# Attention, router and two mixture-of-experts layers on one core: first small loads from ScalarE, noise loads in steps of their own, and a new table for the order of the attention's steps

## The chip, the cores and the metric

The kernel runs on one core of one Trainium2 chip. A core has five engines that run side by side and wait for each other through semaphores: TensorE (PE, matrix products), VectorE (DVE), ScalarE (ACT), GpSimd (POOL) and SyncE (SP, which here only issues transfers). Sixteen DMA engines move the data between the chip's memory and the core's on-chip memory. Every engine works through its own list of instructions strictly in order, so an instruction that waits also holds up all that stands behind it on its engine.

The metric is the device time of one execution in microseconds (us). About 0.3% of it, some 4 us, is what a measurement of this kernel can tell from no change.

## What is computed

The reference has three parts. Only the first, and the routing that follows from it, is touched by the change.

```python
def _attn_ref(q, k, v, g_norm):            # (8, 8, 576, 64) each
    kv = np.einsum('bhsd,bhse->bhde', k, v)
    out = np.einsum('bhsd,bhde->bhse', q, kv)
    rms = np.sqrt(np.mean(out * out, axis=-1, keepdims=True) + 1e-06)
    return (out / rms * g_norm)

x = attn_out.transpose(0, 2, 1, 3).reshape(4608, 512)

def _moe_ref(x, w_gate, w_noise, noise, w1, w2):   # 8 experts, 512 -> 1024 -> 512
    noisy = x @ w_gate + np.log1p(np.exp(x @ w_noise)) * noise
    # the two best experts of each row, weights by softmax over the two,
    # out[row] += weight * (relu(x[row] @ w1[e]) @ w2[e])

def _moe2_ref(x, w_skip, w_gate, w1, w2):  # rows with x @ w_skip > 0: the best expert
    ...                                    # of 8 is added, times its probability
```

## The kernel before

**Three stages.** The attention stage comes first. For each batch b it forms k^T v per head (TensorE, `kv_half`, twice per batch with 4 heads each), then q times that product. The rows of the result are written to `xrows` in memory. Beside it the router picks two experts for each row, in two halves of 4 batches (`route_half`). Then the first expert layer runs, expert by expert, and last the second one. From the first tile of the first expert layer on, the lists of instructions of the two kernels are the same on every engine; the change lies in the stage ahead of it and in the passage between.

**How the attention stage is laid out.** It is a list of 56 steps, `subs`: each is two or three heads of one half batch of q, and after every pair of batches come two steps for the 64 last rows of both. In the steps from `FIRST` = -6 to 56 the loop does, in this order: `run(i, 0)`, `q_transposed` for the step two ahead, `run(i, 1)`, `out_sub` of the step itself, `run(i, 2)`. So `run` has three slots per step, and whatever is filed with `at(step, f, ..., slot)` is written out there. All engines but the order between them are fixed by this: the code is emitted under a manual schedule, so each engine's list is the order in which this loop emits. What is filed where is set by tables of numbers at the top of the file:

- `KV`, `GC`: how many steps ahead of a batch's first step its two `kv_half` run, and where the two parts of `gate_columns` go. `gate_columns` appends 32 columns to the block `kvbd` of the batch, so that the product with q gives the router's logits too: first, TensorE transposes the sums `sw` (L447) and ScalarE copies them out (`kvT`, L449); second, TensorE multiplies them by the gate weights (L453) and ScalarE copies the columns into `kvbd` (L456, two instructions). The batch's first `out_sub` (L486) needs those columns.
- `QTE`, `OSBE`, `SQE`, `LOX`: which engine does each copy of transposed q (`qTs`, L471 or L473), each copy of a result out of PSUM (`osb`, L495 or L497), each square (`sq`, L500 or L502) and the low half of each row (`x`, L538).
- `FIN`, `FINR`: at which later step the normalisation, the logits (`stage3`), the two halves of the rows (`stage4` on ScalarE, L535; `stage5`, L538) and the write of the rows are emitted. Whatever falls behind step 56 goes into the list `late` and is worked off at `f` in the table `TAIL`.
- `WSTEPS`: the first expert's weights; each matrix is loaded (2 MB, `stage`), squared and summed by ScalarE in four pieces (`wjunk`, L175), summed by TensorE (L182, which waits for VectorE's `wsum`, L179), scaled and split.
- `ROUTE`: the 27 parts of the router's first half. The second half and four early tiles of expert 0 are woven together by `EPLAN` and `TAIL`, behind the last steps.
- `LOADS`, `CLEAR`: the remaining first loads, and nine 1 MB writes of zeros to the output.

**Loads.** All loads of the stage are issued by SyncE, in the order of the list. `km` and `vm` (half a batch of k or v, 512 KB each) have three buffers, `qm` has four, `kl`, `vl`, `ql` (the last 64 rows) two. A load of the next half batch is filed `LATER` = 4 steps behind the use that frees its buffer. Behind the first batches SyncE issues the noise of the router, six small loads (L397, L400), and one row of zeros, `null`, to `xrows` (L402).

## Time and profile before

| | us |
|---|---|
| median of 3 runs | 1263.92 |
| lowest and highest of them | 1261.89, 1265.8 |
| the profiled execution, its own time | 1256.98 |
| its span, first to last instruction | 1254.8 |
| TensorE busy in the span | 1176.7 (94%) |
| VectorE, ScalarE, GpSimd busy | 815.3, 656.2, 401.2 |
| granted TensorE clock, mean over the span | 0.98 of full |

The profiled execution is 2.2 us longer than its span and lies 6.9 us below the median of the runs. The busy share of TensorE is an average over the stages: in the expert layers it is at nearly 100%, in the attention stage it is not, and the attention stage is where the granted clock falls below full. So the share by itself doesn't tell what a microsecond saved in the attention stage is worth. What tells it is which wait ends last there, engine by engine, and where the stage hands over to the first full tile of expert 0.

### The profile page before, as it was taken

Reading aid. Unit: us, or ns where it says so; the run is one execution under the profiler, and the core shown is the slowest. Engines: PE = TensorE matmul, PEld = TensorE weight load, DVE = VectorE, ACT = ScalarE, POOL = GpSimd, SP = SyncE. Lnnn points to the kernel's source line nnn. Section 1 sums busy time; section 2 is a strip of 40 time slices with the busy share of each in tenths; the row PEclk is TensorE's granted clock in tenths of the full one; section 3 lists DMA queues with packets and bytes.
Section 4 is the critical chain, followed back from the end, with each engine's and each line's share of the span. In section 5 each row is a group of like instructions: output and inputs, shape, how many; then the busy total and the mean of one; then the engine's idle time right before and its main releaser. Section 6 shows DMA issues by size and latency. Waiting matters only on the chain.

```text
span 1254.8 us, 25287 instructions
## 1 busy us (share of the span) xinstructions
PE 1176.7 (94%) x9341; PEld 838.0 (67%) x9341; DVE 815.3 (65%) x2998; ACT 656.2 (52%) x1187; POOL 401.2 (32%) x477
## 2 busy tenths in 40 slices
PE   6977889999999999999999999999999989999996
PEld 5877777576767676766667576666666666666664
DVE  1777977344786777787777878778787765433321
ACT  2787561356655755574666767557774332222210
POOL 2564552112233232324242233232323331422220
PEclk8998899999999999999999999999999999999998
DMA  9999894678995988799799899979996673795680
GB/s 223 306 308 319 261 257 108 178 210 240 245 292 125 271 270 211 199 244 301 143 305 266 245 328 259 291 209 257 305 295 224 157 215 120 207 328 162 205 247 16
DMA packets 311410, 293.34 MB, mean 234 GB/s; under 512 B 205022, under 2 KB 256222, under 8 KB 307180
## 3 DMA queue, kind: packets, MB, share of 16 engines
q1 hardware_dynamic: 288316, 208.22, 62.7%
q0 software_dynamic: 22384, 82.36, 19.2%
q8 instruction: 75, 1.23, 0.4%
q10 hardware_dynamic: 576, 1.05, 0.3%
q14 instruction: 59, 0.48, 0.1%
HBM read 172.86 MB, written 93.42 MB: 212 GB/s over the span
## 4 chain that ended last, share of the span: by engine, by line
PE 52%; issue 14%; DVE 12%; ACT 11%; POOL 4%; DMA 2%; SPq 2%; another core or an unknown queue 1%; POOLq 0%; ACTq 0%; DVEq 0%
PE b L273 27%; PE a L234 20%; ACT wa L192 2%; ACT wjunk L175 2%; DVE xh L959 2%; ACT hh L242 2%; ACT wb L192 1%; ACT presplit L192 1%; POOL out_dram L1232 1%; PE kvps L421 1%; ACT ysb L1129 1%; DVE x L1133 1%; DVE hl L243 1%; POOL x2r L1187 1%
## 5 line engine op out<-in xcount | busy, mean ns | idle before, releaser
L234 PEld LDWEIGHTS <-wa 128*128 128x128 f16 x5184 | 458.5, 99 | 59.2 <-issue 10.3
L234 PE MATMUL a<-xT,wa 128*128 128x256 f16 (+6 forms) x3648 | 386.8, 266 | 6.7 <-issue 4.5
L273 PE MATMUL b<-wb,hh 128*128 128x512 f16 x1488 | 338.8, 379 | 6.1 <-ACT hh L242 6.1
L273 PEld LDWEIGHTS <-hh 128*128 128x128 f16 x1488 | 140.4, 98 | 167.0 <-ACT hh L242 14.2
L242 ACT ACTIVATE hh<-a 128x512 f16<-128x512 f32 (+5 forms) x186 | 107.1, 578 | 185.1 <-PE a L234 155.2
L243 DVE SCALAR_TENSOR_TENSOR hl<-a,hh 128x512 f16<-128x512 f32 (+5 forms) x186 | 124.9, 674 | 83.4 <-ACT hh L242 77.2
L273 PE MATMUL b<-wb,hl 128*128 128x512 f16 x744 | 175.7, 379 | 0.0
L1075 POOL DMA_INDIRECT xg<-xrows,idxp x67 | 65.6, 978 | 329.5 <-DVE orow L1099 285.2
L273 PEld LDWEIGHTS <-hl 128*128 128x128 f16 x744 | 72.2, 98 | 88.3 <-DVE hl L243 2.9
L1129 ACT ACTIVATE ysb<-b,gate 128x512 f32<-128x512 f32 x73 | 49.7, 681 | 125.8 <-PE b L273 69.0
L234 PE MATMUL a<-x2Tr,wa 128*128 128x256 f16 (+1 forms) x1152 | 109.0, 257 | 2.7 <-DMA x2Tr<-xh 2.7
L1137 POOL DMA_INDIRECT out_dram<-x,oi x67 | 68.3, 1020 | 133.2 <-DVE pi L1045 60.8
L175 ACT ACTIVATE wjunk<-stage 128x1024 bf16<-128x1024 f32 x96 | 101.2, 1054 | 2.0
L193 DVE SCALAR_TENSOR_TENSOR presplit<-stage,wscl,presplit 128x1024 f16<-128x1024 f32 x64 | 80.5, 1278 | 15.9 <-ACT presplit L192 15.0
L1108 POOL DMA_INDIRECT yo<-ydram,gi x67 | 69.9, 1043 | 51.1 <-issue 17.1
L192 ACT ACTIVATE presplit<-stage,wscl 128x1024 f16<-128x1024 f32 x64 | 71.2, 1140 | 18.2 <-DVE wscl L185 16.8
L951 ACT ACTIVATE jk<-x 128x512 bf16<-128x512 f32 x67 | 42.2, 629 | 54.9 <-DVE x L1133 46.7
L958 ACT ACTIVATE xh<-x,x2ss 128x512 f16<-128x512 f32 x67 | 45.4, 714 | 32.7 <-DVE x2ss L141 29.5
L486 PE MATMUL b<-kvbd,qTs 128*128 128x160 f32 x256 | 49.8, 332 | 9.8 <-issue 4.0
L1133 DVE TENSOR_TENSOR x<-ysb,yo 128x512 f32<-128x512 f32 x67 | 46.3, 691 | 18.6 <-ACT ysb L1129 14.4
L1232 POOL DMA_INDIRECT out_dram<-ysb,mrow x16 | 16.3, 1018 | 119.0 <-DVE ysb L1230 119.0
L421 PE MATMUL kvps<-vm,km 128*128 128x128 f32 x256 | 39.7, 320 | 12.7 <-DMA vm<-in_v_dram 9.4
(357 smaller groups left out, 1564.9 us busy)
## 6 DMA issues: line engine op xcount, KB each, us to landing
stage<-in_moe_w_dram SPq DMA_DIRECT2D x32, 2048.0 KB
wsd<-presplit SPq DMA_DIRECT2D x8, 2056.0 KB
ydram<-ysb SPq DMA_DIRECT2D x64, 256.0 KB
wsd<-presplit SPq DMA_DIRECT2D x8, 2048.0 KB
out_dram<-zeros SPq DMA_DIRECT2D x9, 1024.0 KB
km<-in_k_dram SPq DMA_DIRECT2D x16, 512.0 KB
vm<-in_v_dram SPq DMA_DIRECT2D x16, 512.0 KB
qm<-in_q_dram SPq DMA_DIRECT2D x16, 512.0 KB
```

What stands on the lines that cost most here:

```text
L175: A.activation(junk, st[:, F * c:F * c + F], AF.Square, accum_out=acc[:, c:c + 1], **kw)
L192: A.activation(hi[:, d], st[:, d], AF.Copy, scale=sc)
L193: V.scalar_tensor_tensor(lo[:, d], st[:, d], sc, hi[:, d], op0=ALU.mult, op1=ALU.subtract)
L234: PE.matmul(ps[:, i, :], a[:, c, fs], xT[:, b + c, 0:nt], start=(n == 0), stop=(n == 11))
L242: behind[0] = A.activation(hh[:, fsl, 0:nt], ps, AF.Relu).ins
L243: i = V.scalar_tensor_tensor(hl[:, fsl, 0:nt], ps, 0.0, hh[:, fsl, 0:nt], op0=ALU.max, op1=ALU.subtract)
L273: PE.matmul(ps, a[:, f, gsl], b[:, f, :], start=(fs.start == 0 and i == 0), stop=(fs.stop == 8 and a is hl and f == 7))
L1075: G.indirect_dma_start(out=xg[:, g], out_offset=None, in_=xrows, in_offset=bass.IndirectOffsetOnAxis(ap=idx[:, t0 + g:t0 + g + 1], axis=0))
L1108: G.indirect_dma_start(out=yo, out_offset=None, in_=ydram[0:BASE[e], :], in_offset=bass.IndirectOffsetOnAxis(ap=gi[:, g:g + 1], axis=0), b ...
L1129: A.activation(ysb, ps, AF.Copy, scale=gate[:, g:g + 1])
L1133: i = V.tensor_add(x2[:, g], ysb, yos[g])
L1137: s = G.indirect_dma_start(out=out, out_offset=bass.IndirectOffsetOnAxis(ap=oi[:, g:g + 1], axis=0), in_=x2[:, g], in_offset=None, bounds_ ...
```

## The change

It does four things.

1. SyncE's list begins with k and v. The loads that stood ahead of or between them (`gcol`, `kl` and `vl` of the first two batches, the gate weights `gw`) are issued by ScalarE, whose list had nothing but a table load there.
2. The six noise loads and the row of zeros, which SyncE issued in a row behind the third k and v, are filed at the steps of a new table `NOIS`.
3. The tables that set the order of the attention's steps have other numbers.
4. With them, single copies change engine: `OSBE` gives ScalarE 49 of 56 where it had 40, `QTE` 37 where it had 31, `SQE` still 38; `LOX` gives GpSimd 9 of 20 where it had 10.

```diff
-CLEAR = (51, 42, 49, 40, 46, 36, 53, 50, 41)
+CLEAR = (53, 53, 44, 44, 41, 35, 47, 42, 39)
...
-KV, GC = ((6, 3), ((3, 2), (0, 1)))
+KV, GC = ((6, 3), ((1, 0), (0, 0)))
-FIN = ((1, 0), (1, 1), (2, 0), (3, 1), (4, 1), (5, 2))
-FINR = ((1, 2), (1, 2), (2, 1), (3, 2), (6, 0), (8, 0))
+FIN = ((1, 2), (1, 2), (2, 0), (4, 1), (4, 2), (5, 1))
+FINR = ((1, 1), (1, 2), (1, 2), (5, 1), (6, 2), (8, 0))
-LOADS = (0, 1, 1, 1, -2, 20)
+LOADS = (-2, 3, 3, -2, -2, 12)
+NOIS = (16, 17, 18, 20, 21, 22, 23)
...
-WSTEPS = ((4, 12, 12, 13, 14, 15, 15, 15, 16, 18), (20, 24, 26, 27, 29, 29, 30, 35, 35, 38))
+WSTEPS = ((4, 11, 13, 14, 14, 14, 16, 16, 17, 18), (19, 24, 25, 25, 29, 29, 30, 38, 38, 39))
...
     gcol = const.tile([P, 1], F32, name="gcol")
-    SP.dma_start(gcol[0:64], g_norm.rearrange("(p o) -> p o", o=1))
-    SP.dma_start(gcol[64:128], g_norm.rearrange("(p o) -> p o", o=1))
...
-        def load_rest(nm, src, pb):
+        def load_rest(nm, src, pb, eng=SP):
...
-        load_rest("k", k, 0)
-        load_rest("v", v, 0)
+        load_rest("k", k, 0, A)
+        load_rest("v", v, 0, A)
         load_kv(1)
         load_q(0)
+        for c in range(2):
+            A.dma_start(gcol[64 * c:64 * c + 64], g_norm.rearrange("(p o) -> p o", o=1))
...
-        SP.dma_start(gw[:, :, 0:8], w_gate.rearrange("(c p) e -> p c e", p=P))
-        SP.dma_start(gw[:, :, 8:16], w_noise.rearrange("(c p) e -> p c e", p=P))
+        A.dma_start(gw[:, :, 0:8], w_gate.rearrange("(c p) e -> p c e", p=P))
+        A.dma_start(gw[:, :, 8:16], w_noise.rearrange("(c p) e -> p c e", p=P))
...
+        def load_noise(a, bl):
+            if bl is None:
+                SP.dma_start(noi[:, a, 0:16].rearrange("p (b r) e -> p b (r e)", r=4),
+                             nv[a, :, 0:512].rearrange("b (p r) e -> p b (r e)", r=4))
+            else:
                 SP.dma_start(noi[64 * bl:64 * bl + 64, a, 16:18],
                              nv[a, bl:4:2, 512:S].rearrange("b p e -> p b e"))
-        SP.dma_start(xrows[0:1, :].rearrange("o (p w) -> (o p) w", w=16), null)
+        def null_row():
+            SP.dma_start(xrows[0:1, :].rearrange("o (p w) -> (o p) w", w=16), null)
...
+        for step, (f, *args) in zip(NOIS, [(load_noise, a, bl) for a in range(2) for bl in (None, 0, 1)] + [(null_row,)]):
+            at(step, f, *args)
```

The first place is the start of SyncE's list. `km`, `vm` and `qm` are half batches of k, v and q, numbered by buffer. Before:

```order
L129 DMA gcol_82<-in_g_norm_dram 64x1
L130 DMA gcol_82<-in_g_norm_dram 64x1
L324 DMA km_142<-in_k_dram 128x4x256
L324 DMA vm_144<-in_v_dram 128x4x256
L330 DMA kl_146<-in_k_dram 64x8x64 x2
L330 DMA vl_149<-in_v_dram 64x8x64 x2
L324 DMA km_152<-in_k_dram 128x4x256
L324 DMA vm_154<-in_v_dram 128x4x256
L337 DMA qm_156<-in_q_dram 128x8x128
L363 DMA gw_169<-in_moe_w_gate_dram 128x4x8
L364 DMA gw_169<-in_moe_w_noise_dram 128x4x8
```

Now:

```order
L323 DMA km_140<-in_k_dram 128x4x256
L323 DMA vm_142<-in_v_dram 128x4x256
L323 DMA km_150<-in_k_dram 128x4x256
L323 DMA vm_152<-in_v_dram 128x4x256
L336 DMA qm_154<-in_q_dram 128x8x128
L336 DMA qm_192<-in_q_dram 128x8x128
L323 DMA km_194<-in_k_dram 128x4x256
L323 DMA vm_196<-in_v_dram 128x4x256
L323 DMA km_235<-in_k_dram 128x4x256
L323 DMA vm_237<-in_v_dram 128x4x256
```

Eight small loads have left the front of the list: two of `gcol`, four halves of `kl` and `vl`, two of `gw`. The fourth k and v, `km_235` and `vm_237`, come directly behind the third, with no noise between.

The second place is ScalarE around the first step of the second batch (`kvbd_178` is that batch's block, `x_349` and `x_337` are the high half of the first rows). Before:

```order
L495 ACTIVATE osb<-b 128x480
L449 ACTIVATE kvT<-small 128x512
L317 ACTIVATE kvbd_178<-sw 64x4x64
L471 ACTIVATE qTs<-a 128x384
L500 ACTIVATE sq<-osb 128x384
L471 ACTIVATE qTs<-a 128x384
L535 ACTIVATE x_349<-osb 128x8x2x64
L456 ACTIVATE kvbd_178<-small 64x8x16 x2
```

Now:

```order
L476 ACTIVATE qTs<-a 128x384
L500 ACTIVATE osb<-b 128x480
L505 ACTIVATE sq<-osb 128x384
L454 ACTIVATE kvT<-small 128x512
L500 ACTIVATE osb<-b 128x320
L461 ACTIVATE kvbd_178<-small 64x8x16 x2
L540 ACTIVATE x_337<-osb 128x8x2x64
```

The gate columns (L456, now L461) moved ahead of the copy of the rows (L535, now L540), and the copy `kvT` moved from far ahead of them to one copy ahead of them. On TensorE the transposes that feed `kvT` moved with it: they now stand in the step ahead of the batch's first one.

The third place is VectorE behind the last step, where the second half of the router begins (`L<-zt` are the last logits, `na` begins the router, `x_1996` and `x_1993` are the low halves of the same rows, `x_2142` those of the very last ones). Before:

```order
L506 TENSOR_REDUCE ss<-sq 128x4
L538 TENSOR_TENSOR x_1996<-osb,x_1996 128x8x2x64
L528 SCALAR_TENSOR_TENSOR rmsa<-rinv 128x8
L529 SCALAR_TENSOR_TENSOR rmsa<-ss,rmsa 128x8
L530 SCALAR_TENSOR_TENSOR rinv<-rmsa,rinv 128x8
L552 TENSOR_TENSOR zt<-osb,rinv 128x128
L557 TENSOR_REDUCE L<-zt 128x16
L582 SCALAR_TENSOR_TENSOR na<-L 128x144
L588 TENSOR_SCALAR w<-u 128x144
L538 TENSOR_TENSOR x_2142<-osb,x_2142 128x512
```

Now:

```order
L511 TENSOR_REDUCE ss<-sq 128x4
L242 SCALAR_TENSOR_TENSOR hle<-a,hhe 128x512
L533 SCALAR_TENSOR_TENSOR rmsa<-rinv 128x8
L534 SCALAR_TENSOR_TENSOR rmsa<-ss,rmsa 128x8
L535 SCALAR_TENSOR_TENSOR rinv<-rmsa,rinv 128x8
L557 TENSOR_TENSOR zt<-osb,rinv 128x128
L562 TENSOR_REDUCE L<-zt 128x16
L587 SCALAR_TENSOR_TENSOR na<-L 128x144
L543 TENSOR_TENSOR x_1993<-osb,x_1993 128x8x2x64
L593 TENSOR_SCALAR w<-u 128x144
```

The large `x` moved from ahead of the logits to behind `na`, and the last one (`x_2142`) left VectorE for GpSimd.

## Rows read from the trace of the kernel before

**Rows 1.** The page: the span, and TensorE's busy share and clock in 40 slices.
```profile
span 1254.8 us, 25287 instructions
...
PE   6977889999999999999999999999999989999996
...
PEclk8998899999999999999999999999999999999998
```

**Rows 2.** Windows: length, busy us (x instructions) by engine, granted clock, DMA share, GB/s.
```profile
20.00:23.00 3.00, 0.67 (x6) 0.70 (x7) 0.00 (x0) 0.49 (x2) 0.00 (x0) 1.00 0.56 107
...
139.00:147.00 8.00, 8.00 (x55) 7.45 (x51) 7.83 (x14) 2.88 (x10) 3.79 (x3) 0.57 1.05 326
...
24.00:115.00 91.00, 77.39 (x566) 71.04 (x565) 64.69 (x154) 66.90 (x145) 50.46 (x44) 0.91 1.09 304
60.00:100.00 40.00, 32.83 (x254) 29.85 (x253) 30.86 (x70) 34.16 (x73) 27.25 (x23) 0.96 1.09 301
```

**Rows 3.** TensorE's waits up to 210 us: waiter, releaser, total us, times, longest.
```profile
PE small L447 <- DVE sw L431: 6.2, 6, 1.6
```

**Rows 4.** Timeline of SyncE, beginning: start us, us taken to issue, line, transfer.
```profile
0.83 0.61 SPq L129 DMA_DIRECT2D gcol<-in_g_norm_dram  x1
...
2.12 0.59 SPq L324 DMA_DIRECT2D km<-in_k_dram  x1
...
15.87 0.51 SPq L397 DMA_DIRECT2D noi<-in_moe_noise_dram  x1
...
20.82 0.52 SPq L402 DMA_DIRECT2D xrows<-null  x1
```

**Rows 5.** DMA queues, 0 to 40 us: what they moved, one value for each us.
```profile
GB/s 0 0 0 62 197 342 369 281 202 211 303 348 345 305 213 223 274 217 327 363 243 74 5 54 321 386 332 250 230 263 129 336 377 327 315 250 185 159 108 291
```

**Rows 6.** Timeline of TensorE: start us, us, line, tiles, form [idle before, what ended it].
```profile
22.33 2.88 PE L421 MATMUL kvps<-vm,km 128*128 128x128 f32 x16 [2.42 <-DMA xrows<-null]
...
40.42 1.94 PE L486 MATMUL b<-kvbd,qTs 128*128 128x160 f32 x6 [1.93 <-POOL sq L502]
...
44.42 1.95 PE L421 MATMUL kvps<-vm,km 128*128 128x128 f32 x16
...
65.01 0.38 PE L182 MATMUL small<-wsum,ones 128*128 128x1 f32 x2 [1.58 <-DVE wsum L179]
...
67.58 3.65 PE L421 MATMUL kvps<-vm,km 128*128 128x128 f32 x16 [1.04 <-DMA vm<-in_v_dram]
...
79.42 1.05 PE L486 MATMUL b<-kvbd,qTs 128*128 128x160 f32 x6 [2.48 <-ACT kvbd L456]
...
117.48 1.05 PE L486 MATMUL b<-kvbd,qTs 128*128 128x160 f32 x6 [3.18 <-issue]
...
143.33 3.38 PE L421 MATMUL kvps<-vm,km 128*128 128x128 f32 x16
```

**Rows 7.** Timeline of ScalarE ahead of 40.42 us, and ahead of 117.48 us.
```profile
39.78 0.54 ACT L456 ACTIVATE kvbd<-small 64x128 f32<-64x128 f32 x2
...
116.84 0.54 ACT L456 ACTIVATE kvbd<-small 64x128 f32<-64x128 f32 x2
```

**Rows 8.** ScalarE by line, 0 to 180 us: busy us, mean ns | idle before, releaser.
```profile
L495 ACT ACTIVATE osb<-b 128x480 f32<-128x480 f32 (+1 forms) x39 | 20.4, 524 | 9.5 <-PE b L486 9.1
L500 ACT ACTIVATE sq<-osb 128x384 f32<-128x384 f32 (+1 forms) x37 | 18.2, 491 | 8.7 <-DVE osb L497 7.7
...
L471 ACT ACTIVATE qTs<-a 128x384 f32<-128x384 f32 (+1 forms) x31 | 13.3, 431 | 0.2
...
L175 ACT ACTIVATE wjunk<-stage,gcol 128x1024 bf16<-128x1024 f32 x4 | 4.6, 1141 | 0.1
```

**Rows 9.** Timeline of VectorE behind the last step.
```profile
182.69 1.23 DVE L538 TENSOR_TENSOR x<-osb,x 128x1024 f16<-128x1024 f32 x1
...
187.09 0.23 DVE L588 TENSOR_SCALAR w<-u 128x144 f32<-128x144 f32 x1 [1.30 <-ACT u L585]
187.61 0.69 DVE L538 TENSOR_TENSOR x<-osb,x 128x512 f16<-128x512 f32 x1 [0.29 <-ACT x L535]
```

More of the change, by code (lines that the diff above doesn't have):

```diff
@@ L35 @@
 BEGIN = 3
-CLEAR = (51, 42, 49, 40, 46, 36, 53, 50, 41)
+CLEAR = (53, 53, 44, 44, 41, 35, 47, 42, 39)
 AHEAD = [{(CUT + 2, 0): "g", (CUT + 2, 1): "a", (CUT + 3, 0): "s", (CUT + 3, 1): "b"},
          {(CUT + 3, 2): "g", (CUT + 4, 0): "s", (CUT + 4, 1): "a"}]
-KV, GC = ((6, 3), ((3, 2), (0, 1)))
-FIN = ((1, 0), (1, 1), (2, 0), (3, 1), (4, 1), (5, 2))
-FINR = ((1, 2), (1, 2), (2, 1), (3, 2), (6, 0), (8, 0))
-LOX = 'GVVGGGGGGVVVVVGVGGVV'
+KV, GC = ((6, 3), ((1, 0), (0, 0)))
+FIN = ((1, 2), (1, 2), (2, 0), (4, 1), (4, 2), (5, 1))
+FINR = ((1, 1), (1, 2), (1, 2), (5, 1), (6, 2), (8, 0))
+LOX = 'VVGGVGGVGVVVVGVGVGVG'
 SQS = (1, 0)
-LOADS = (0, 1, 1, 1, -2, 20)
-ROUTE = (9, 12, 15, 15, 17, 21, 22, 22, 23, 23, 23, 30, 31, 31, 33, 35, 36, 39, 40, 45, 48, 53, 57, 58, 59, 59, 61)
+LOADS = (-2, 3, 3, -2, -2, 12)
+NOIS = (16, 17, 18, 20, 21, 22, 23)
+ROUTE = (10, 13, 14, 15, 18, 21, 21, 21, 22, 22, 23, 30, 30, 30, 32, 34, 35, 37, 41, 45, 51, 54, 59, 59, 59, 60, 62)
 LATER = 4
 URGENT = 500
-QTE = 'VVAVVAAAVAVVAAVVAAAAVAVVAAAVAVVVVAVAAVAAVAAAVVAAAAAAAVVV'
-OSBE = 'AVAAVVAAVAAVVVAAAVAAAAVVAVVAAAAAAAAAAAAAVAAAAAVAAAVAAAVA'
-SQE = 'AAGGAGGAAGAGGGAAGGAGAAGAAGGAAGGAAAAAGAGAAAAAAAAAAAAAAAAA'
-WSTEPS = ((4, 12, 12, 13, 14, 15, 15, 15, 16, 18), (20, 24, 26, 27, 29, 29, 30, 35, 35, 38))
-EPOOL = 39
+QTE = 'AAVAAAAVVVAAVAVAVVVAAAVAAVVAVAAVVAAAAAAAAAVAVAAVAAAAAVAA'
+OSBE = 'AAAAAAVAAVAAAAAAAAAAAAAVAVAAAAAAAAAAAVAAAAAAAAAAVAAVAAAA'
+SQE = 'AGGGAGAAGAAGGGGAAGAGAAAAAGGAGGGGAAAAAAAAAAAAAAAAAAAAGAAA'
+WSTEPS = ((4, 11, 13, 14, 14, 14, 16, 16, 17, 18), (19, 24, 25, 25, 29, 29, 30, 38, 38, 39))
+EPOOL = 40
 OHB = 3
-EPLAN = (((48, 0), (50, 0), (54, 1), (55, 1), (55, 1), (55, 2)), ((51, 1), (52, 2)), (), ())
-TAIL = 'r 0 0 r f r r 2 f r r r r 1 1 f f 2 f r 1 r 1 r r r f 1 f r r r r r r 3 r 2 2 1 r 2 r 2 2 r r 3 3 2 r r 3 3 r 3 3 3'
+EPLAN = (((48, 0), (48, 0), (54, 1), (56, 0), (56, 0), (56, 2)), ((50, 2),), (), ())
+TAIL = 'r 0 f f r 1 r f r 2 2 r r r 0 1 r r 1 1 f r f 1 r 1 r r f r r r 1 2 r r r r r 2 2 r 2 r f 3 3 2 r r r r 3 3 3 3 2 3 3'
 T2 = 5
@@ L325, in load_kv @@
                 QT[nm, b, hh] = t
-        def load_rest(nm, src, pb):
+        def load_rest(nm, src, pb, eng=SP):
             t = ld.tile([P, H, DH], F32, name=f"{nm}l")
             for bl in range(2):
-                SP.dma_start(t[64 * bl:64 * bl + 64],
+                eng.dma_start(t[64 * bl:64 * bl + 64],
                              src[2 * pb + bl, :, 512:576, :].rearrange("h p d -> p h d"))
@@ L395, in moe_kernel @@
         nv = noise.rearrange("(a b s) e -> a b s e", a=2, b=4)
-        for a in range(2):
-            SP.dma_start(noi[:, a, 0:16].rearrange("p (b r) e -> p b (r e)", r=4),
-                         nv[a, :, 0:512].rearrange("b (p r) e -> p b (r e)", r=4))
-            for bl in range(2):
+        def load_noise(a, bl):
[3 more added lines that the diff above has]
+            else:
                 SP.dma_start(noi[64 * bl:64 * bl + 64, a, 16:18],
                              nv[a, bl:4:2, 512:S].rearrange("b p e -> p b e"))
-        SP.dma_start(xrows[0:1, :].rearrange("o (p w) -> (o p) w", w=16), null)
+        def null_row():
+            SP.dma_start(xrows[0:1, :].rearrange("o (p w) -> (o p) w", w=16), null)
         def two_blocks(ap, o):
```

## The prediction

> **What bounds the kernel now.** I read the page's slices first: TensorE is below nine tenths in the first six slices of 31 us and at or near full in the rest, and the granted clock falls below full in the same early part [rows 1]. So the attention stage has slack and the expert layers have none. Since the lists from the first full tile of expert 0 on are the same before and after, the change is worth exactly as much as it moves that hand-over, and I count every term as a shift of it.
>
> Next I read who ends TensorE's waits in that stage. There is no single culprit. The third k^T v starts at 22.33 us after 2.42 us of idle ended by a transfer; the first product of the 2nd, 4th and 6th batch waits 1.93, 2.48 and 3.18 us; the sum for the weights 1.58 us [rows 6]; the transposes of `sw` 6.2 us in six waits [rows 3]. The releasers named for the 1.93 and the 3.18 ("POOL sq", "issue") are not the real ones: ScalarE's list ends the gate columns at 40.32 us and 117.38 us, 0.1 us ahead of the two products [rows 6, 7].
>
> Last I read what else is full. From 24 to 115 us the DMA engines show a share of 1.09 at 304 GB/s [rows 2]: they never rest, although TensorE waits for a load only once there, 1.04 us at 67.58 us [rows 6]. So loads run just ahead of use, and are the next thing to be late. ScalarE is busy 34.16 of 40 us between 60 and 100 us [rows 2], 85%.
>
> **The change part by part.**
>
> *Start of the loads.* SyncE's first k is issued at 2.12 us behind two `gcol` loads and would now go at 0.83 us [rows 4]: -1.3 us for the first product and for the whole front of loads. The loads given to ScalarE lie in its idle start and cost nothing there as long as they end ahead of its first copy; if the queue is slow, they cost about what one issue takes, 0.6 us [rows 4]. The third k^T v needs eight half batches plus the small loads. These bytes still have to pass, and DMA was already moving 200 to 370 GB/s from 4 to 20 us [rows 5], so the earlier issue of the later ones gains nothing beyond the 1.3. What does go is the noise behind them. Between 0 and all of the 2.42 us idle is due to that; I take 0.5, since the data of k and v fill the stretch up to 20 us. Together -1.8 (0 to -3.7).
>
> *Front of the loads behind that.* While SyncE issued noise and `null` (15.87 to 21.34 us [rows 4]), DMA ran dry: 74, 5 and 54 GB/s in the three us from 21 [rows 5], share 0.56 from 20 to 23 us [rows 2]. The fourth k and v now stand directly behind the third, so about 2 us of DMA time come back; the front is 3.3 us ahead with the 1.3. The Trainium skill ("DMA: Bandwidth & Descriptors", Issuing engines are not separate DMA queues) says that issuing from several engines saves only the time to issue, usually small beside the transfer. The row disagrees for tiny loads in a row, whose issue left the engines dry; by the rule this start would be worth about nothing and the sum 1.8 us less.
>
> *Noise in steps 16 to 23.* The same issues, 5.5 us of SyncE as above, now stand between loads in the full stretch. Where SyncE is held back by full queues anyway they are hidden; without that cover they delay what is queued behind them, the k and v of the sixth batch and the row writes. I take +0.5 (0 to +5.5).
>
> *Transposes of `sw`.* They move from the step of the product that feeds them to two or more steps behind it, so five of the six waits go: 6.2 x 5/6 = -5.2. In return `kvT` now has only three transposes and one product of two or three heads to hide behind, with `osb` (0.52) and `sq` (0.49 [rows 8]) ahead of it on ScalarE. I take 0.4 us of new wait in seven batches, +2.8 (0 to 7 x 1.0). Together -2.4 (-5.2 to +1.8).
>
> *Gate columns.* In the 2nd, 4th and 6th batch the columns now go ahead of the large copy of the rows. What remains between the last product and the next one is `osb` 0.52, sometimes `sq` 0.49, and two copies of about 0.27 (0.54 for both [rows 7]), some 1.5 us. TensorE's own gate product and two transposes hide a part of that; I count half and take 0.8 us of wait each: 1.93 + 2.48 + 3.18 - 2.4 = -5.2 (0 to -7.6).
>
> *Sum for the first weights.* Two squares of 1.14 us [rows 8] now stand in front of TensorE's sum in the same slot, where one square and one `sq` stood: 2 x 1.14 - (1.14 + 0.49) = +0.65, say +0.7, on top of the 1.58.
>
> *Behind the last step.* VectorE's chain from the last logits to the row numbers loses `x` of 1.23 us, which moves into a wait of 1.30 us for ScalarE, and the 0.69 us one, which goes to GpSimd [rows 9]: -1.9 (0 to -1.9). TensorE's early tiles there are the same amount of work in either order.
>
> *Clock.* After some of these waits the granted clock falls: 0.57 from 139 to 147 us [rows 2], between the levels of 1.2 and 2.4 GHz, and sixteen products take 3.38 us where they take 1.95 [rows 6]. Fewer waits should leave fewer such stretches; I take -1.0 (0 to -3).
>
> *Copies on ScalarE.* 9 more `osb` and 6 more `qTs` are 9 x 0.524 + 6 x 0.431 = 7.3 us [rows 8], taken off VectorE. ScalarE has room outside 60 to 100 us. There the net is three `osb` and one `sq` more and one `qTs` less, 1.6 us, which would make it 35.8 of 40. I take +1.0 (0 to +5.1, if all ten net copies up to the 28th step lie on the path).
>
> The sum is -1.8 + 0.5 - 2.4 - 5.2 + 0.7 - 1.9 - 1.0 + 1.0 = -10.1. Not all of it can be kept: of the terms about -5 fall ahead of 105 us, and the loads there are only 3.3 - 0.5 = 2.8 us earlier while DMA has no gap. I give 2 us back to that: -8. Against its own time the profiled execution would go from 1256.98 to 1249. That execution lies 6.9 below the median, and the measured figure is a median, so I set 1263.92 - 8 = **1256**; its own spread, from -4 to -11, is 1253 to 1260.
>
> **The rivals.**
>
> *More of it comes true.* All waits named go, the clock stays up and the loads hold pace: -1.8 - 5.2 - 7.6 - 3 + 0.7 - 1.9 = -18.8, of which 4 or 5 go to the loads: about 1250. For it: the waits are separate. Against: the new order leaves less distance to `kvT`.
>
> *Loads set the pace, and waits change places.* With DMA at 1.09 from 24 to 115 us, noise in the way at half its price (+2.7) eats the 2.8 us of lead, so nothing is won ahead of 105 us. Behind it remain the sixth batch's columns (-2.4) and the chain at the end (-1.9), less the copies on ScalarE (+1.7): -2.6, 1261, no change that can be told. For it: the 1.04 us wait shows a load already late. Against: it is one wait in 91 us.
>
> *ScalarE becomes the bound; slower.* It works in order, and TensorE needs its `osb` to free PSUM. If the ten net copies of the first 28 steps go straight onto the path (+5.1), `kvT` is late in every batch (+1.8 net), the columns gain only 1.0, the sum costs 0.7, and the start and end keep -1.8 and -1.9: +2.9. The other five copies, at 0.45, add 2.2: +5.1, 1269. It decides from where ScalarE is busy above some 38 of the 40 us between 60 and 100; by rows it would be at 35.8, which speaks against it.
>
> **How the numbers follow.** Forecast 0.48, more of it 0.12, loads 0.24, ScalarE 0.16. 0.3% is 3.8 us and about what a measurement can tell. Faster by more: the forecast, except a tenth of it, and the first rival: 0.43 + 0.12 = 0.55, and 0.02 from the second. Within: 0.22 of the loads, 0.05 of the forecast, 0.02 of ScalarE: 0.29. Slower: 0.14. The range leaves out half of the first rival and most of the third: 1248 to 1267.
>
> **What would show it.** Right: the first k^T v at about 7 us and the third near 20.5; no dry us behind 20; waits of the 2nd, 4th and 6th batch's first product below 1 us; few waits for `sw`; the sum for the first weights waiting over 2 us; the row numbers 6 to 10 us earlier. Wrong: TensorE waiting for `vm` in several batches (loads), ScalarE above 38 of 40 us or TensorE waiting for `osb` and `kvT` again and again (ScalarE), or an early tile that isn't there when TensorE comes to it, since its load by transposition now stands behind 2 MB of zeros.

## The result

The changed kernel is slower: 1283.34 us median of six runs (1269.54 to 1290.21) beside 1264.8 us (1261.89 to 1270.18) for the kernel before, a ratio of 1.0112, 95% interval 1.0077 to 1.0148. The ratios leave out executions in a slow state, here the one of 1290.21 us, and are not the quotient of two medians (1.0147 here); the only profile of a_g21_w below fell in such an execution (1391.77 us) and is not read. The forecast was 1256, the range ended at 1267. The profiled execution took 1275.99 us, its span is 1274.1, 19.3 above that of before.

The page of the changed kernel, to be laid beside [rows 1]: span, and TensorE's busy share and granted clock in 40 slices.

```profile
span 1274.1 us, 25289 instructions
...
PE   6788788999999999999999999999989999999996
...
PEclk8987789999999999999999999999989999999998
```

Ahead of the expert layers' long stretch of nines the first seven slices are below nine tenths, and the clock is now lower in slices 3 to 6. How much of the loss lies there is read from the first matmul of the first full tile, from which on all engines' lists are the same in both kernels. TensorE's timeline there, first of before, then of after (the second row is cut by the window that was asked for and counts 48 of the same 96 matmuls):

```profile
226.11 10.64 PE L234 MATMUL a<-xT,wa 128*128 128x256 f16 x96 [1.06 <-DMA xT<-xg]
```

```profile
238.13 7.07 PE L233 MATMUL a<-xT,wa 128*128 128x256 f16 x48 [2.00 <-DMA xT<-xg]
```

So 12.0 of the 19.3 us are lost ahead of this hand-over. The windows up to it (columns as in [rows 2]), before and after:

```profile
0.00:226.11 226.11, 182.85 (x1543) 159.66 (x1543) 153.90 (x390) 125.25 (x272) 106.22 (x126) 0.92 0.93 252
```

```profile
0.00:238.13 238.13, 192.12 (x1543) 167.58 (x1544) 153.09 (x383) 129.78 (x287) 105.39 (x125) 0.87 0.89 240
```

This pair is the main reading of the whole case. TensorE has the same 1543 matmuls in both. Its idle time is 226.11 - 182.85 = 43.26 us before and 238.13 - 192.12 = 46.01 after: 2.75 us more. The other 9.27 us are the same matmuls taking longer, at a mean granted clock of 0.87 in place of 0.92. A second pair of executions on one chip (b_again is the kernel before, a_again the changed one) says the same:

```profile
0.00:228.36 228.36, 185.48 (x1543) 162.40 (x1544) 153.15 (x379) 124.69 (x272) 106.39 (x126) 0.90 0.92 250
```

```profile
0.00:239.14 239.14, 195.10 (x1542) 170.56 (x1543) 151.03 (x365) 129.58 (x287) 105.52 (x125) 0.86 0.87 238
```

Here 1.16 us are idle time and 9.62 longer matmuls. The change hardly added idle time; it moved it to places behind which the clock is low.

TensorE's waits up to 210 us, after (waiter, releaser, total us, times, longest):

```profile
PE small L458 <- ACT kvT L454: 12.1, 6, 3.5
PE kvps L426 <- DMA vm<-in_v_dram: 8.4, 1, 8.4
PE small L181 <- DVE wsum L178: 6.6, 2, 3.4
PE small L452 <- DVE sw L436: 3.0, 3, 2.6
...
PE a L233 <- DMA xTe<-xge: 2.0, 1, 2.0
```

The waits for `sw` are halved against [rows 3], 3.0 in place of 6.2 us, and a group that did not exist before stands on top: 12.1 us for `kvT`. Where that falls, on TensorE's timeline after, beside [rows 6]:

```profile
8.37 3.75 PE L426 MATMUL kvps<-vm,km 128*128 128x128 f32 x16 [8.37 <-DMA vm<-in_v_dram]
...
23.02 3.62 PE L426 MATMUL kvps<-vm,km 128*128 128x128 f32 x16
...
39.86 1.05 PE L491 MATMUL b<-kvbd,qTs 128*128 128x160 f32 x6 [0.44 <-issue]
...
63.61 0.56 PE L181 MATMUL small<-wsum,ones 128*128 128x1 f32 x2 [3.40 <-DVE wsum L178]
...
73.23 0.56 PE L452 MATMUL small<-ident,sw 64*128 64x64 f32 x4
...
78.36 1.43 PE L458 MATMUL small<-gbd,kvT 128*128 128x32 f32 x8 [3.54 <-ACT kvT L454]
80.48 1.94 PE L491 MATMUL b<-kvbd,qTs 128*128 128x160 f32 x6 [0.21 <-issue]
...
123.01 1.94 PE L491 MATMUL b<-kvbd,qTs 128*128 128x160 f32 x6 [0.21 <-issue]
...
141.72 0.33 PE L452 MATMUL small<-ident,sw 64*128 64x64 f32 x2 [2.64 <-DVE sw L436]
...
146.79 1.92 PE L458 MATMUL small<-gbd,kvT 128*128 128x32 f32 x8 [3.45 <-ACT kvT L454]
```

The first product of the 2nd, 4th and 6th batch (39.86, 80.48, 123.01) hardly waits any more, as forecast, but the gate's own product right ahead of it does. ScalarE's timeline ahead of the 3.54 us:

```profile
74.76 0.49 ACT L476 ACTIVATE qTs<-a 128x384 f32<-128x384 f32 x1
75.15 0.62 ACT L540 ACTIVATE x<-osb 128x512 f16<-128x512 f32 x1
75.67 0.56 ACT L500 ACTIVATE osb<-b 128x480 f32<-128x480 f32 x1
76.26 0.52 ACT L505 ACTIVATE sq<-osb 128x384 f32<-128x384 f32 x1
76.69 1.13 ACT L191 ACTIVATE wa<-stage,wscl 128x1024 f16<-128x1024 f32 x1
77.73 0.57 ACT L454 ACTIVATE kvT<-small 128x512 f32<-128x512 f32 x1
```

The transposes that `kvT` copies end at 73.79, `kvT` starts at 77.73: in between ScalarE works off what stands ahead of it in its list, a split of `wa` of 1.13 us among it. Ahead of the 3.45 us it is another thing that stands there:

```profile
145.70 0.31 ACT L528 ACTIVATE rinv<-ss,eps 128x16 f32<-128x16 f32 x1 [1.74 <-DVE ss L511]
...
146.16 0.58 ACT L454 ACTIVATE kvT<-small 128x512 f32<-128x512 f32 x1
```

ScalarE stood idle for 1.74 us there, since `rinv`, next in its list, waited for VectorE's `ss` (both belong to the normalisation of the rows), and `kvT` had to wait with it. The windows show the clock around the waits (columns as above):

```profile
20.00:23.00 3.00, 2.37 (x12) 2.16 (x11) 0.00 (x0) 1.39 (x4) 0.00 (x0) 0.65 1.12 342
...
60.00:100.00 40.00, 31.39 (x204) 28.63 (x202) 25.60 (x60) 32.33 (x66) 19.23 (x17) 0.79 0.95 260
...
64.00:68.00 4.00, 4.00 (x17) 3.93 (x18) 3.06 (x14) 2.29 (x4) 2.32 (x3) 0.50 1.11 351
80.00:84.00 4.00, 3.79 (x16) 3.51 (x15) 0.91 (x3) 2.91 (x8) 2.13 (x1) 0.50 0.87 271
144.00:156.00 12.00, 9.21 (x39) 8.72 (x40) 10.18 (x19) 3.37 (x10) 5.83 (x3) 0.50 0.73 218
```

Behind the 3.40 us of idle time that end at 63.61 and the 3.54 that end at 78.36 four microseconds each pass at 0.50 (the 1.2 GHz level), and from 144 to 156 us, around the 3.45 us, all twelve. The low clock is in the second execution too: a_again has 0.50 from 64 to 68, from 80 to 84 and from 148 to 160 us. From 60 to 100 us ScalarE is busy 32.33 of 40 us, where the two executions of before have 34.16 [rows 2] and 30.78, and DMA's share is 0.95, not 1.09 and 1.10: ScalarE is no fuller than it was, and the loads are less so.

The DMA queues after, 0 to 40 us, one value for each us, beside [rows 5]:

```profile
GB/s 0 4 101 308 310 176 330 205 306 307 300 298 259 281 289 240 212 346 347 346 351 349 326 288 237 192 192 252 351 345 315 287 193 88 295 193 155 366 381 391
```

The loads begin a microsecond earlier and the dry microseconds from 21 on are gone, but the first product of k and v starts at 8.37 us (8.31 in the trace of before).

### The profile page after: what moved, and what is told of

It reads as the page before. It is cut to its first block, busy times and chain, and to the rows that moved or that the text cites. A ratio compares the mean times of both kernels' runs of the same rounds, so it can differ in the third digit from the quotient of the medians.

```text
span 1274.1 us, 25289 instructions
## 1 busy us (share of the span) xinstructions
PE 1190.6 (93%) x9341; PEld 846.9 (66%) x9341; DVE 815.5 (64%) x2984; ACT 660.7 (52%) x1202; POOL 401.3 (31%) x476
## 3 DMA queue, kind: packets, MB, share of 16 engines
q8 instruction: 75, 1.23, 0.4%
## 4 chain that ended last, share of the span: by engine, by line
PE 54%; DVE 12%; issue 11%; ACT 11%; DMA 5%; POOL 3%; another core or an unknown queue 2%; SPq 0%; POOLq 0%; DVEq 0%; ACTq 0%
PE b L272 25%; PE a L233 20%; PE kvps L426 2%; PE b L491 2%; ACT wa L191 2%; ACT hh L241 2%; ACT presplit L191 1%; ACT wjunk L174 1%; DVE xh L966 1%; DVE x L1140 1%; DMA x2T<-xh 1%; ACT ysb L1136 1%; PE small L458 1%; DVE hl L242 1%
## 5 line engine op out<-in xcount | busy, mean ns | idle before, releaser
L491 PE MATMUL b<-kvbd,qTs 128*128 128x160 f32 x256 | 53.4, 350 | 1.5 <-issue 1.4
L536 POOL TENSOR_TENSOR osb<-osb,rinv 128x1024 f32<-128x1024 f32 (+1 forms) x20 | 37.6, 1882 | 41.8 <-DVE rinv L535 39.9
```

The source lines that it names most:

```text
L491: PE.matmul(po[:, i, :], qT[:, i, :], kvb[b % 4][:, h0 + i, :], start=True, stop=True)
```

## The experiments

Every ratio is to the kernel before in runs on the same chip and in the same set; the median of before was 1250.5 us in the first set (b_gc to a_loads), 1261.1 in the second (b_again to a_gc21), 1261.5 in the third (a_g21_lox, a_g21_w, a_g21_tail, b_g21_loads), 1266.8 in the fourth (a_g21_all, b_g21_act, b_g21_loads2, b_g21_ld_lds) and 1251.8 in the last (a_g21_cop, a_g21_most). "Tile" is the start of the first full tile in the profiled execution, in us, and the waits are TensorE's up to 210 us. In `GC` the first pair says how many steps ahead of a batch's first product, and at which place in the step, the transposes of `sw` stand, the second pair the same for the product that needs `kvT`.

| run | ratio, 95% interval | tile | waits for kvT | for sw |
|---|---|---|---|---|
| b_gc | 1.0066, 1.0039 to 1.0092 | 236.70 | 15.0 | 2.4 |
| a_gc | 1.0127, 1.0074 to 1.0180 | 235.79 | none | 13.7 |
| a_copies | 1.0123, 1.0081 to 1.0166 | 241.29 | 15.3 | 4.9 |
| a_loads | 1.0106, 1.0067 to 1.0145 | 239.60 | 13.8 | 3.0 |
| b_again | one run, 1257.96 us | 228.36 | none | 5.8 |
| a_again | 1.0123, 1.0083 to 1.0163 | 239.14 | 12.1 | 3.1 |
| b_gc21 | 0.9997, 0.9968 to 1.0025 | 227.02 | 0.5 | 4.0 |
| a_gc21 | 1.0087, 1.0060 to 1.0114 | 235.66 | 1.9 | 11.5 |
| a_g21_lox | 1.0051, 1.0026 to 1.0076 | 227.33 | 1.2 | 12.1 |
| a_g21_w | 1.0055, 1.0026 to 1.0083 | - | - | - |
| a_g21_tail | 1.0072, 1.0049 to 1.0096 | 234.46 | 1.5 | 11.9 |
| a_g21_all | 1.0045, 1.0016 to 1.0074 | 232.45 | 0.6 | 14.2 |
| a_g21_cop | 1.0106, 1.0067 to 1.0145 | 237.97 | 1.0 | 14.1 |
| a_g21_most | 1.0064, 1.0028 to 1.0101 | 227.23 | 0.6 | 10.0 |
| b_g21_act | 0.9986, 0.9961 to 1.0010 | 225.58 | 0.5 | 4.2 |
| b_g21_loads | 0.9963, 0.9934 to 0.9993 | 225.03 | 0.5 | 6.0 |
| b_g21_loads2 | 0.9962, 0.9938 to 0.9985 | 227.09 | 0.5 | 6.0 |
| b_g21_ld_lds | 0.9957, 0.9936 to 0.9978 | 225.19 | 0.5 | 4.2 |

**Which part loses.** One run puts the gate's new steps alone on the kernel before, three put one part of the changed kernel back.

```diff
b_gc, on the kernel before
-KV, GC = ((6, 3), ((3, 2), (0, 1)))
+KV, GC = ((6, 3), ((1, 0), (0, 0)))
a_gc, on the changed kernel: the same, the other way
a_copies, on the changed kernel: QTE, OSBE, SQE, LOX of before
a_loads, on the changed kernel: SyncE issues gcol, kl, vl, gw again; noise ahead of the steps again
```

> The kernel before with the new places of the gate columns, GC = ((1, 0), (0, 0)), alone. Theory (late kvT): TensorE's 6.2 us of waits for sw go, waits of 8 us or more for kvT come, the hand-over goes from 226.1 to 231 or later, and the time by 4 us or more. Rival (ScalarE too full): with the old copies kvT is early enough; waits for kvT stay under 4 us and the hand-over within 2 us of 226.1, or ahead of it.

> The changed kernel with the old places of the gate columns, GC = ((3, 2), (0, 1)); all else is changed. Theory (late kvT): the changed kernel's 12.1 us of TensorE waits for kvT, and the slow clock behind them, come from the new GC alone. Then these waits fall below 2 us, the hand-over to the first full tile (238.1 us in the changed kernel, 226.1 before) comes back by 8 us or more, and the time by as much. Rival (ScalarE too full): kvT is late because ScalarE has 15 copies more; then the waits only move to the columns (L461) or osb, and the hand-over moves by under 4 us.

> The changed kernel with the old choice of engine for each copy, square and low half (QTE, OSBE, SQE, LOX); all else is changed. Rival (ScalarE too full): ScalarE's queue ahead of kvT is short again, the waits for kvT fall from 12.1 us to under 5, the hand-over comes 6 us or more earlier. Theory (late kvT by its place): waits stay at 8 us or more, the hand-over moves by under 4 us.

> The changed kernel with all small loads back on SyncE and the noise behind the third k and v, as before; the tables stay changed. If the loads are part of the loss (noise in steps delaying the k and v behind it), the hand-over comes 3 us or more earlier than 238.1. If the new start is worth what was forecast, it comes 1 to 4 us later. If the eight transfers in flight set the start either way, it moves by under 1.5 us.

The waits of b_gc up to 210 us:

```profile
PE small L453 <- ACT kvT L449: 15.0, 7, 5.5
...
PE small L447 <- DVE sw L431: 2.4, 3, 1.7
```

This one number pair makes the kernel before 0.66% slower, and the wait for `kvT` appears with it, in an order that has the old copies and loads. Its window up to the first full tile:

```profile
0.00:236.70 236.70, 188.50 (x1542) 164.22 (x1543) 155.38 (x399) 125.51 (x272) 106.25 (x126) 0.88 0.88 241
```

Against the first row of before above, 5.65 us are longer matmuls and 4.9 us idle time. Neither the copies nor the loads of before make the changed kernel better: "ScalarE is too full" falls with a_copies, which takes copies off it and waits 15.3 us for `kvT` all the same. And the old `GC` does not repair the changed kernel (a_gc), against the theory that was set for it: there the wait passes to `sw`, 13.7 us, and the ratio stays at 1.0127. So the late `kvT` alone is not the whole loss.

**Room for kvT.** b_again and a_again are the two kernels unchanged, for their traces on one chip; the other two move the transposes a step and a half ahead of the product that needs `kvT`.

```diff
b_gc21 on the kernel before, a_gc21 on the changed kernel
+KV, GC = ((6, 3), ((2, 1), (0, 0)))
```

> The kernel before, unchanged, for its trace beside the others of this chip. If the loss of the changed kernel lies in the lists ahead of the first full tile, the first product of the first full tile starts here within 2 us of 226.1, and TensorE's clock from 100 to 200 us is near 0.88. If the two profiled executions shown so far differ for another reason (the chip, the execution), it starts up to 10 us away from there.

> The changed kernel, unchanged, for its trace and time beside the others of this chip. Theory (its own order of work is late): ratio to the kernel before 1.007 to 1.015, first full tile at 237 to 240 us, TensorE waiting 10 to 14 us for kvT. Rival (the execution of the first trace was an odd one): first full tile before 233 us.

> The kernel before with the transposes of sw two steps and the columns' product one step ahead of a batch's first product, both at place 0 or 1 of the step, so that the copy kvT has a step more than in the changed kernel. Theory (what the changed kernel lost is the wait for kvT, which stood behind other copies in ScalarE's list): kvT waits fall from 15.0 to 3 to 6 us, waits for sw stay under 5 us, first full tile at 224 to 230 us, ratio 0.995 to 1.002. Rival (the gate's steps lose as much wherever they are put, since the wait moves to sw or the columns): waits of gate steps together stay above 12 us, first full tile after 233 us, ratio 1.004 or more.

> The changed kernel with the same one edit. Theory: kvT waits fall from 12.1 to 3 to 5 us and the first full tile comes at 229 to 232 us (what is left over the kernel before is the sum for the first weights and the early tile's load), ratio 1.000 to 1.006. Rival: first full tile after 235 us and ratio over 1.008, the wait having moved to sw or to the columns.

b_again starts the first full tile 2.25 us behind the first execution of before, a little more than expected, a_again 1.0 behind the first of after, so the late hand-over is no oddity of one execution. From 60 to 100 us b_again has a clock of 0.83, where the first execution had 0.96 [rows 2]: the clock of one stretch varies that much within one kernel, and only what stands in both executions should be read from it. In b_gc21 0.5 us of waits for `kvT` are left and the 0.66% are gone: the theory of the late copy held on the order of before. On the changed kernel the same edit takes off less than a third of the loss (1.0123 to 1.0087, with intervals that overlap): `kvT` falls to 1.9 us, even further than expected, but `sw` rises to 11.5, so the rival was right there. The longest of these, 5.0 us, is explained by VectorE's and GpSimd's timelines in a_gc21:

```profile
152.86 1.35 DVE L673 TENSOR_TENSOR ohp<-iop,ph 128x1152 f16<-128x1152 f16 x1
...
154.59 5.88 DVE L673 TENSOR_TENSOR ohp<-iop,ph 128x1152 f16<-128x1152 f16 x1
...
161.05 0.40 DVE L436 TENSOR_TENSOR sw<-kvps,sw 64x256 f32<-64x256 f32 x1
```

```profile
154.43 2.12 POOL L543 TENSOR_TENSOR x<-osb,x 128x1024 f16<-128x1024 f32 x1
156.52 2.73 POOL L676 TENSOR_TENSOR rhs<-ohv,oht 128x720 f16<-128x720 f16 x2
```

(`ohp` and `rhs` are what the router's next products are made of, `x` is the low half of a row.) The same `ohp` takes 1.35 us at 152.86 and 5.88 at 154.59, where GpSimd runs `x` and two `rhs` without a gap until 159.25; `sw` stands behind it. The Trainium skill ("SBUF — State Buffer", SBUF: two separate sides) says that a GpSimd operation that reads SBUF and a VectorE operation with two inputs in SBUF share a pair of ports under an exclusive lock, held for a whole instruction. The trace agrees with the lock, and here VectorE did not get in between GpSimd's three instructions either. It does not always stand back so long: in the same trace an `ohp` that starts at 147.21, beside a GpSimd `osb` that ends at 148.10, takes 2.10 us, and the `rhs` that follows on GpSimd takes 2.50 us, where the two above take 2.73 together: there VectorE did get in between.

**Three more places of the changed order, and the loads on the order of before.**

```diff
a_g21_lox, on a_gc21
-LOX = 'VVGGVGGVGVVVVGVGVGVG'
+LOX = 'VVGGVGGVGVVVVVVGVGVG'
a_g21_w, on a_gc21: WSTEPS of before
a_g21_tail, on a_gc21: EPLAN and TAIL of before
b_g21_loads, on b_gc21: both changes to the loads (ScalarE issues, NOIS)
```

> The changed kernel with the gate's steps at (2, 1) and (0, 0), and one letter of LOX (entry 13) turned from G to V, so that one subtraction of 128x1024 goes from GpSimd to VectorE and GpSimd's row x, rhs, rhs falls apart. Theory (VectorE's ohp of 5.88 us, 1.35 elsewhere, stands still while GpSimd runs three in a row, and the last batch's sw stands behind it): that ohp falls under 3 us, the last and longest wait for sw from 5.0 to under 2.5 us, first full tile 2 to 4 us earlier than 235.7, ratio 1.0055 to 1.0075. Rival (ohp is long by itself there, or the wait is taken up by what stands next): ohp stays above 5 us or the first full tile moves by under 1 us, ratio 1.008 to 1.010.

> The changed kernel with the gate's steps at (2, 1) and (0, 0), and the steps of the first weights (WSTEPS) as before. Theory (the new steps make TensorE wait for the first sum, and put the split of wb ahead of sw in VectorE's list): waits for the two sums from 6.5 to 4.7 to 5.0 us, the wait for sw of 3.5 us near 138 us under 1.5 us, first full tile 2 to 4 us earlier than 235.7, ratio 1.005 to 1.007. Rival (these waits hide others): first full tile within 1 us, ratio 1.008 to 1.010.

> The changed kernel with the gate's steps at (2, 1) and (0, 0), and the places of the early tiles and the order behind the attention's last step (EPLAN, TAIL) as before. Theory (the second early tile is placed ahead of the landing of its rows, and VectorE's hle of it holds up the last part of the routing): the wait of 2.7 us for xTe gone, first full tile 1.5 to 4 us earlier than 235.7, ratio 1.005 to 1.0075. Rival (another wait behind the last step takes its place): first full tile within 1 us, ratio 1.008 to 1.010.

> The kernel before with the gate's steps at (2, 1) and (0, 0), and with both changes to the loads: ScalarE issues the first small ones, SyncE begins with k, the noise is loaded in steps 16 to 23. As predicted for the start (1.8 us earlier, half a microsecond of it given back by the noise, no dry time at 20 to 23 us): first product of k and v near 7 us, third near 20.5, first full tile at 224 to 226 us, ratio 0.997 to 0.999. Rival (what is in flight at a time is bounded, so that the order of issue alone gains nothing at the start): first product at 8.2 to 8.5 us, first full tile at 226.5 to 229 us, ratio 0.9995 to 1.003.

In a_g21_lox `ohp` is down to 1.34 us, but the wait for `sw` stays at 4.9, against the expectation. What moved to VectorE is held now, with GpSimd's two `rhs` beside it:

```profile
149.32 4.09 DVE L543 TENSOR_TENSOR x<-osb,x 128x1024 f16<-128x1024 f32 x1
153.34 1.34 DVE L673 TENSOR_TENSOR ohp<-iop,ph 128x1152 f16<-128x1152 f16 x1
```

```profile
149.60 2.73 POOL L676 TENSOR_TENSOR rhs<-ohv,oht 128x720 f16<-128x720 f16 x2
```

`x` of this size takes 1.23 us in [rows 9]; here it ends 1.08 us behind GpSimd's row, as `ohp` above ended 1.22 behind it: it is the overlap that holds VectorE, not the instruction. The first full tile came 8.3 us earlier than in a_gc21, but 2.9 of that stand already at 103 us, ahead of the edit. In a_g21_tail the wait for `xTe`, 2.7 us in a_gc21, is gone as expected. Each of the three edits brings the point estimate down by 0.15 to 0.36%; the intervals overlap that of a_gc21, so no single one of them is shown.

b_g21_loads is the surprise: 0.9963, faster than both kernels. Its first product of k and v starts at 8.35 us, no earlier than before, as the rival said; the gain the theory had set (0.997 to 0.999) is there nevertheless, and a little more. Its third product starts at 22.21 us, hardly earlier than before, but behind a second one that took 3.77 us for its 16 matmuls. Where the second takes 2.05 us, the third starts at 20.75 us (b_g21_loads2, the same kernel), 20.87 (b_g21_act) and 20.81 (b_g21_ld_lds), with 0.3 to 0.8 us of waiting; with the old loads it is 22.33, 22.64 (b_again) and 21.93 (b_gc21), with 2.1 to 2.6 us. So the new start is worth 1.1 us or more at the third product, and b_g21_act shows that ScalarE's issue alone is enough for it.

**What is left.** a_g21_all puts the three edits together; the two others put back, beside WSTEPS, EPLAN and TAIL, either the engines of the copies (a_g21_cop) or the steps of finishing and routing with LOX (a_g21_most). The loads are taken apart on b_gc21.

```diff
a_g21_all, on a_gc21: LOX as in a_g21_lox; WSTEPS, EPLAN, TAIL of before
a_g21_cop, on a_gc21: WSTEPS, EPLAN, TAIL, QTE, OSBE, SQE, LOX of before
a_g21_most, on a_gc21: WSTEPS, EPLAN, TAIL, FIN, FINR, LOX, ROUTE of before
b_g21_act, on b_gc21: ScalarE issues; noise ahead of the steps
b_g21_loads2: b_g21_loads again
b_g21_ld_lds, on b_g21_loads: LOADS of the changed kernel
```

> The changed kernel with four edits together: the gate's steps at (2, 1) and (0, 0), entry 13 of LOX on VectorE, and WSTEPS, EPLAN and TAIL as before. Theory (the loss of the changed kernel is the sum of these places, each of which moved the ratio by 0.0015 to 0.0036 alone): ratio 0.998 to 1.002, first full tile at 224 to 229 us. Rival (the parts overlap, and something else in the changed order holds the rest): ratio 1.003 to 1.007, first full tile at 230 to 234 us.

> The changed kernel with the gate's steps at (2, 1) and (0, 0), WSTEPS, EPLAN and TAIL as before, and the engines of the copies (QTE, OSBE, SQE, LOX) as before; the steps of finishing and routing stay those of the change. If the rest of the loss lies in the copies (VectorE, with its sums and the row of GpSimd's operations ahead of sw, is what sw waits for): waits for sw from 14 to 4 to 6 us, first full tile at 225 to 228 us, ratio 0.995 to 0.999. If it lies in the steps: waits for sw above 10 us, ratio 1.002 to 1.006.

> The changed kernel with the gate's steps at (2, 1) and (0, 0), WSTEPS, EPLAN and TAIL as before, and the steps of finishing and routing (FIN, FINR, ROUTE, with LOX, which goes by them) as before; the engines of the other copies stay those of the change. If the rest of the loss lies in these steps (they put x, rinv and the routing's large operations ahead of sw in VectorE's list): waits for sw from 14 to 4 to 6 us, first full tile at 225 to 228 us, ratio 0.995 to 0.999. If it lies in the copies: waits for sw above 10 us, ratio 1.002 to 1.006.

> As the kernel before it, but with only ScalarE's issue of the first small loads; the noise is loaded in one piece ahead of the steps, as before. If the gain is ScalarE's, ratio 0.995 to 0.999 and no dry DMA at 20 to 23 us; if it is the noise in steps, ratio 0.999 to 1.002, with TensorE waiting 1 to 2.5 us for the third product of k and v near 22 us.

> The kernel before with the gate's steps at (2, 1) and (0, 0) and both changes to the loads, once more, on another set of runs. Theory (the loads part of the change gives 0.2 to 0.5% where the order of the attention's steps is left as it was): ratio 0.994 to 0.999. Rival (the 0.9963 of the first set was its luck): 0.999 to 1.002.

> As b_g21_loads2, and with the steps of the other loads (LOADS) of the changed kernel, so that the whole of the change's loads stands on the order of before. If these steps are part of the gain, ratio 0.993 to 0.997; if they are neutral, 0.995 to 0.999; if the q loads ahead of the steps take room from k and v, 0.999 to 1.003 and the third product of k and v after 22.5 us.

a_g21_all stays at 1.0045: the parts overlap, as the rival said, and waits for `sw` of 14.2 us remain. a_g21_cop has as many (14.1) with the old copies, and a_g21_most, with the old steps, still waits 10.0 us. The kernels themselves tell more. a_g21_most differs from b_g21_ld_lds (4.2 us) in `QTE`, `OSBE`, `SQE`, `CLEAR` and `EPOOL` alone, and a_g21_cop differs from it in `FIN`, `FINR`, `ROUTE`, `CLEAR` and `EPOOL` alone. Their waits for `sw` from 50 to 100 us, in the order a_g21_most, a_g21_cop, b_g21_ld_lds:

```profile
PE small L452 <- DVE sw L436: 6.2, 3, 4.8
```

```profile
PE small L452 <- DVE sw L436: 8.5, 3, 5.2
```

```profile
PE small L451 <- DVE sw L435: 1.0, 1, 1.0
```

The first write of zeros is issued at 117.91 us or later in all three, and `EPOOL` acts later still, so these waits come from the other tables: on the order of before the engines of the copies bring them by themselves, and so do the steps of finishing and routing. In a_gc21, where WSTEPS is the change's too, they are 2.0 us in this stretch. So a table put back among the others can bring a wait of its own, and runs of this kind do not divide the loss. The ratio of a_g21_cop, 1.0106, lies above both ranges that were set for it. How the time divides is not settled: the ratios (1.0064, 1.0106, 0.9957) are from two chips, `CLEAR` and `EPOOL` were never put back alone, and a_g21_most stays at 1.0064 although its first full tile starts at 227.23.

The loads' gain stands in three runs: 0.9963, 0.9962 on another set, and 0.9957 with all of the change's load steps, with each interval below 1. The interval of b_gc21, the same without the loads, overlaps theirs. ScalarE's issue alone gives 0.9986, an interval that holds 1. What the noise does shows in the DMA queues, one value for each us from 0, first of b_g21_act, then of b_g21_loads2:

```profile
GB/s 0 6 126 237 329 190 304 220 293 302 302 300 262 280 290 249 212 328 348 257 65 13 126 382 373 306 199 250 226 240 377 378 310 288 207 127 131 158 312 310
```

```profile
GB/s 0 6 117 231 336 187 296 221 296 301 301 300 263 277 292 245 216 324 349 346 350 348 311 211 248 295 342 343 341 302 257 154 137 134 52 309 330 344 286 384
```

The dry patch at 20 to 22 us (65, 13, 126; in the kernel before 74, 5, 54 [rows 5]) is there with the noise ahead of the steps and gone with the noise in steps; ScalarE's issue does not remove it. Where the 0.4% are won the traces do not show, beyond the 1.1 us at the third product: the first full tile starts at 225.03, 227.09 and 225.19 us in these three runs, at 227.02 in b_gc21. **So the change's loads gain 0.4% on the order of before with `GC` at (2, 1) (b_g21_ld_lds), and that kernel beats both; what the change does beyond that costs 1.6 to 1.7% (1.0112 and 1.0123, each over 0.9957, from different sets).** On the changed order the gain does not show: with the old loads (a_loads) it stands at 1.0106, within the interval of the changed kernel.

## Why the prediction was wrong

The sign was wrong, and so was the range. Step by step:

- **That only the hand-over counts** was right for 12.0 of the 19.3 us. The other 7.3 come behind it, with the same lists: the same 7799 matmuls are busy for 998.50 us in place of 993.90, and 2.7 us more are idle. Of a_again against b_again, on one chip, 10.8 us stand at the first full tile and 17.8 at the end. One execution's hand-over does not tell its time either: b_gc and a_g21_most, on one chip, took 1258.56 and 1259.00 us and started the first full tile at 236.70 and 227.23. Why stays open. (Of the "first six slices" of [rows 1] the second already stands at nine tenths; nothing in the sum hangs on it.)
- **Transposes of `sw`** is the first of the two steps that failed most, by its half on `kvT`. The waits for `sw` lost 3.2 us instead of 5.2, and `kvT` was priced at seven times 0.4, 2.8 us in all with 7.0 as the most; it took 12.1 in six waits (15.0 in seven with the new `GC` alone, b_gc), 9.3 us more than taken. The price rested on an `osb` and a `sq` ahead of `kvT`. At 78 us a split of 1.13 us, `x`, `qTs` and three small ones stood there too, and at 146 us a `rinv` that itself waited for VectorE. All of them stand in ScalarE's list, whose order the tables fix before a run.
- **Clock** is the second, 10.3 us off: -1.0 by the reasoning that fewer waits mean fewer slow stretches, against +9.3 us of longer matmuls at the first full tile (9.6 in the second pair). A wait of 3.45 us close behind one of 2.64 (ending at 146.79 and 141.72 us) left the whole stretch from 144 to 156 us at 0.50, and in a_again, behind the same wait, the one from 148 to 160. No other term held the slower matmuls behind a wait, and this one had their sign wrong.
- **Gate columns** came true by itself: 0.44, 0.21 and 0.21 us where 0.8 each was taken, 6.7 us less. It was not kept, since the same chain of copies is now waited for one product earlier.
- **Sum for the first weights**: +0.7 taken, 6.6 - 4.7 = +1.9 measured (4.7 in b_again too).
- **Behind the last step**: -1.9 taken. From the last logits to the row numbers it was 26.96 us before and is 30.55 after, +3.6. VectorE's timeline, of before, then of after, where the second early tile is in the way:

```profile
185.16 0.63 DVE L582 SCALAR_TENSOR_TENSOR na<-L 128x144 f32<-128x144 f32 x1
...
211.95 0.17 DVE L702 TENSOR_SCALAR idx<-iacc 128x10 int32<-128x10 f32 x1
```

```profile
194.04 0.63 DVE L587 SCALAR_TENSOR_TENSOR na<-L 128x144 f32<-128x144 f32 x1
...
202.30 0.69 DVE L242 SCALAR_TENSOR_TENSOR hle<-a,hhe 128x512 f16<-128x512 f32 x1 [2.91 <-ACT hhe L241]
...
224.42 0.17 DVE L707 TENSOR_SCALAR idx<-iacc 128x10 int32<-128x10 f32 x1
```

  This is the sign that the prediction's list of what would make it wrong ended with (`xTe`, the transposed rows of an early tile, not there, 2.0 us); it stood in no term.
- **Start of the loads**: -1.3 for the first product taken, nothing measured (8.37 against 8.31 us). SyncE's first k left 1.3 us earlier, but the second k and v left with it, and by the first product 1.55 MB had passed where 1.31 had before (the sum of the values per us). In the program the transfers behind the eighth wait for the one eight before them (SyncE's first q load, which needs no buffer to come free, waits 2.3 us for a landing of k), so the queue fills no faster. For the third product 20.5 us was forecast, and three of the four runs of the loads on the order of before come close (20.75 to 20.87). With the noise still ahead of the steps b_g21_act waits 0.80 us there, not 2.42, so most of that wait was not the noise's. In the changed kernel it starts at 23.02 all the same, behind a second product that took 3.58 us where it takes 2.05 in before. The Trainium skill ("DMA: Bandwidth & Descriptors", Issuing engines are not separate DMA queues), by which issuing from several engines saves little, agrees with ScalarE's part: 0.9986, not told from nothing.
- **Front of the loads** (dry patch gone) was right, 342 GB/s from 20 to 23 us where it was 107 [rows 2]; **noise in steps** was taken as a cost of 0.5, and the point estimates say it gains (0.9986 to 0.9962; the intervals overlap).
- **Copies on ScalarE**: 32.33 of 40 us busy, not the 35.8 worked out (TensorE got through less in this stretch, 204 matmuls for 254), and a_copies shows no gain from taking them back.
- **The rival that ended slower** (1269, still 14 us short) had the mechanism half: `kvT` late in every batch. It priced that at 1.8 us net and put its cause into a full ScalarE. The place in the list decided, not the load on the engine.

## What to carry to other kernels

Where a change moves an instruction in a list that is worked off in order, read the rows that stand between its input and it on *every* engine of its chain, and price the wait by all of them, not by the two usual ones. Price a TensorE wait with the slow stretch behind it: compare busy time for the same count of matmuls, not only idle time. And take a change with several parts apart: here loads that gain 0.4% on the order of before came together with an order that costs more than 1%. When one part put back repairs nothing, another may bring the same wait by itself.
